# S5 scan and gated MLP on one core: a recurrence over tokens becomes a recurrence over token pairs

## The chip, the cores and the metric

The kernel runs on one core of a Trainium2 chip. The metric is the device time of one execution in microseconds (us). The engines are called as in the profile: PE is TensorE's matmuls (PEld its weight loads), DVE is VectorE, ACT is ScalarE, POOL is GpSimd, and SP is SyncE, which here only issues transfers.

## What is computed

```python
xn = layernorm(x)                              # x: 2048 tokens x 448
# branch A: a diagonal complex recurrence over the tokens, D = P = 448
Lam_bar = exp(exp(log_dt) * Lambda)            # per state p
B_bar = ((Lam_bar - 1) / Lambda)[:, None] * B  # q * B, q one complex number per state
h[t] = Lam_bar * h[t-1] + B_bar @ xn[t]
s[t] = 2 * real(C @ h[t]) + xn[t] * Dskip
# branch B: layer norm again, 448 -> 1792 -> 448
g = silu(gelu(layernorm(xn) @ w1 + b1) @ w2 + b2)
out = x + s * g
```

## The kernel before

The 2048 tokens are cut into NG = 4 groups of 512, and a group into four tiles of 128 tokens. All weights and all of x stay in SBUF. Each group goes through these steps.

- **Layer norm** (L333 to L369). Statistics on DVE; both norms (xn and the norm of xn) follow from one variance by a few short instructions (L346 to L358, on DVE for group 0, on POOL afterwards), and the scaling is on DVE for group 0, on ACT afterwards. The result is turned to columns by PE transposes in group 0 (L384) and by DMA transposes (L73) afterwards.
- **bu** (L500, L506): `B @ xn` for a block of 128 states, real and imaginary part, each four matmuls of 512 columns (K = 448 padded to 512). The 448 states are three full blocks (i = 0, 1, 2) and one block i = 3 that holds 64 real and 64 imaginary rows.
- **ssm**: a block's input is turned by a table `WT` of cosines and sines, multiplied by q (L521 to L523), so that what is left is a real decay; a DVE scan over 512 tokens (L530) runs it, once each for the real and the imaginary part; ACT casts the result (L535), and a table `VT` turns it back to h (L564 to L566). POOL turns the last column into the start value of the next group (L548 to L560).
- **mm1** (L574): a pair of 128-row blocks of the MLP's hidden layer, eight matmuls of 512 columns into two PSUM banks, then gelu on ACT (L581). Seven pairs make a group.
- **mm2** (L589, L591): for one tile, fourteen matmuls of 448 columns and one for the bias, into bank 6; tanh on ACT (L593); `g_sb` = (tanh + 1) * psum on DVE (L594).
- **ym** (L601, L603): for one tile, seven matmuls of 448 columns `C @ h` and four short ones for Dskip, into bank 7; DVE multiplies by `g_sb` (L606) and adds x (L607), and SP sends the tile out.

Nothing of this is in the order of the loops. Every step is a task of a planner (`Plan`) with an engine, the buffers it reads and writes, an assumed duration and a priority. The planner plays the tasks through with the assumed durations, and each engine's program is what came out: a fixed row in which each instruction waits for the semaphores of its inputs. What an engine does while it waits for one instruction is therefore nothing. The tables are made in the first stretch, block by block, with Sin on ACT (L438, L440), and ACT loads another table when it goes from Sin to gelu or back.

## Time and profile before

| what | us |
| --- | --- |
| median of 3 runs | 207.49 (207.39 to 207.61) |
| the profiled execution, its own time | 207.9 |
| its span, first to last instruction | 206.1 |
| PE busy | 159.0 (77%) |
| DVE busy | 154.5 (75%) |
| ACT busy | 122.5 (59%) |
| POOL busy | 44.1 (21%) |

The shares are averages over a kernel with two very different stretches, so the page's part 2, the span in forty slices, is to be read beside them: the row PE says in tenths how busy the engine was in a slice, the row PEclk which clock it was granted (9 is full speed).

### The profile page before, as it was taken

What the parts mean: (1) busy time and instruction counts of PE and PEld (TensorE: products, weight loads), DVE (VectorE), ACT (ScalarE), POOL (GpSimd) and SP (SyncE); (2) the same over time, 40 slices, a digit from 0 to 9 for tenths busy, and PEclk for the clock granted to TensorE, in tenths of its full rate; (3) what the DMA queues carried; (4) which work ended last, traced back from release to release, by engine and by line L of the source; (5) the groups of instructions that cost most, each with busy time, mean ns of one, the idle gap of its engine ahead of it and who ended that gap; (6) DMA issues with size and microseconds to landing.
All of it is one profiled execution on the core that took longest, in us unless ns stands there. A gap on an engine that the chain in (4) does not pass through costs nothing.

```text
span 206.1 us, 2551 instructions
## 1 busy us (share of the span) xinstructions
PE 159.0 (77%) x816; PEld 77.7 (38%) x816; DVE 154.5 (75%) x306; ACT 122.5 (59%) x163; POOL 44.1 (21%) x142
## 2 busy tenths in 40 slices
PE   0399339932900086999999999999999999979992
PEld 0274114310300032444544445555444555435551
DVE  6877995756699986839695857999967999935333
ACT  2366999999223089859978666543677361681110
POOL 4028200101305988850202013030410000000000
PEclk9999967996795558799999999999999999999998
DMA  5999990000000024224130500211200010100100
GB/s 168 275 282 310 285 133 0 2 0 0 0 0 2 0 50 99 60 51 104 42 73 26 102 0 0 51 48 25 70 0 3 0 36 9 48 5 0 39 28 22
DMA packets 25041, 12.61 MB, mean 61 GB/s; under 512 B 17854, under 2 KB 24675, under 8 KB 25028
## 3 DMA queue, kind: packets, MB, share of 16 engines
q1 hardware_dynamic: 24596, 10.84, 22.8%
q0 software_dynamic: 416, 1.61, 2.4%
q8 instruction: 6, 0.10, 0.2%
q14 instruction: 7, 0.06, 0.1%
q10 hardware_dynamic: 16, 0.00, 0.0%
HBM read 6.66 MB, written 1.84 MB: 41 GB/s over the span
## 4 chain that ended last, share of the span: by engine, by line
PE 61%; ACT 18%; POOL 6%; DMA 5%; DVE 4%; issue 2%; SPq 2%; DVEq 0%; ACTq 0%
PE psum L589 21%; PE psum L574 18%; PE psum L601 10%; PE psum L500 8%; DMA w_sb<-in_B_w_dram 4%; ACT L581 3%; ACT gT L581 2%; SPq L74 2%; ACT xn_sb L369 2%; ACT L438 2%; PE psum L603 2%; PE psum L591 1%; ACT tb L440 1%; PE psum L506 1%; ACT L440 1%
## 5 line engine op out<-in xcount | busy, mean ns | idle before, releaser
L589 PE MATMUL psum<-w_sb,gT 128*128 128x448 bf16 x224 | 50.7, 383 | 25.1 <-DVE g_sb L594 16.7
L574 PE MATMUL psum<-xn2T,w_sb 128*128 128x512 bf16 x224 | 53.9, 392 | 7.5 <-ACT gT L581 7.2
L589 PEld LDWEIGHTS psum<-w_sb,gT 128*128 128x128 bf16 x224 | 22.9, 105 | 50.4 <-issue 24.2
L581 ACT ACTIVATE gT<-psum 128x1024 bf16<-128x1024 f32 x28 | 28.6, 1024 | 16.2 <-PE psum L574 16.0
L574 PEld LDWEIGHTS psum<-xn2T,w_sb 128*128 128x128 bf16 x224 | 21.6, 101 | 33.7 <-ACT gT L581 8.2
L530 DVE TENSOR_TENSOR_SCAN s_f<-cw,cur,v_sb 128x512 f32<-128x512 f32 x21 | 25.9, 1270 | 0.6
L500 PE MATMUL psum<-xnT,BT 128*128 128x512 bf16 x96 | 23.3, 387 | 2.1 <-DMA xnT<-xn_sb 2.1
L601 PE MATMUL psum<-CT,h_sb 128*128 128x448 bf16 x112 | 23.8, 352 | 0.0
L593 ACT ACTIVATE th<-psum 128x448 f32<-128x448 f32 x16 | 8.6, 540 | 22.3 <-PE psum L591 22.3
L369 ACT ACTIVATE xn_sb<-x_all,lnw 128x448 bf16<-128x448 bf16 x24 | 16.7, 751 | 8.2 <-POOL lnw L358 8.2
L504 ACT ACTIVATE u_sb<-psum 128x1024 bf16<-128x1024 f32 x12 | 12.2, 1021 | 8.5 <-PE psum L500 6.6
L594 DVE SCALAR_TENSOR_TENSOR g_sb<-th,psum 128x448 bf16<-128x448 f32 x16 | 9.8, 612 | 9.1 <-ACT th L593 9.1
L535 ACT ACTIVATE s_b<-s_f 128x1024 bf16<-128x1024 f32 x12 | 12.6, 1051 | 6.0 <-DVE s_f L530 6.0
L601 PEld LDWEIGHTS psum<-CT,h_sb 128*128 128x128 bf16 x112 | 11.0, 98 | 10.6
L606 DVE TENSOR_TENSOR t<-psum,g_sb 128x448 bf16<-128x448 f32 x16 | 9.9, 619 | 6.3 <-PE psum L603 6.3
L500 PEld LDWEIGHTS psum<-xnT,BT 128*128 128x128 bf16 x96 | 9.2, 99 | 13.5 <-issue 3.0
L564 DVE TENSOR_TENSOR pa<-s_b,VT 128x1024 bf16<-128x1024 bf16 x12 | 8.2, 686 | 7.6 <-ACT s_b L535 7.6
L548 POOL TENSOR_TENSOR cwk<-s_f,rot 128x1 f32<-128x1 f32 x9 | 2.3, 252 | 50.8 <-DVE s_f L530 42.3
L568 DVE TENSOR_TENSOR pa<-s_b,QT 128x1024 bf16<-128x1024 bf16 x4 | 2.8, 692 | 10.2 <-ACT s_b L539 10.2
L396 PE MATMUL psum<-ident,gT 128*128 128x128 bf16 x28 | 3.6, 269 | 8.6 <-DMA gT<-in_A_B_re_dram 6.2
L333 DVE BATCH_NORM_STATS2 lnst<-x_all 128x6 f32<-128x448 bf16 x16 | 9.2, 614 | 0.6 <-DMA x_all<-in_A_x_dram 0.6
L522 DVE TENSOR_TENSOR pb<-u_sb,WT 128x1024 bf16<-128x1024 bf16 x12 | 8.2, 685 | 0.9 <-ACT u_sb L504 0.9
(134 smaller groups left out, 219.0 us busy)
## 6 DMA issues: line engine op xcount, KB each, us to landing
out_dram<-o_sb SPq DMA_DIRECT2D x16, 112.0 KB, 1.7
w_sb<-in_B_w_dram POOLq DMA_DIRECT2D x2, 784.0 KB, 7.9
w_sb<-in_B_w_dram SPq DMA_DIRECT2D x2, 672.0 KB, 7.8
x_all<-in_A_x_dram SPq DMA_DIRECT2D x3, 448.0 KB, 9.2
x_all<-in_A_x_dram SPq DMA_DIRECT2D x2, 224.0 KB, 2.9
gT<-in_A_B_re_dram SPq DMA_DIRECT2D x1, 336.0 KB, 4.3
...
```

Of the source, the lines that this page charges most:

```text
L333: dve(lambda e, t=t, tl=tl: e.bn_stats(lnst[:, tl, :], x_all[:, t, :]), [f"x{t}"], [f"st{tl}"], 0.56, prio)
L369: act(lambda e: e.activation(dst, x_all[:, t, :], ACT.Identity, bias=nb, scale=rs), rd, [key], 0.66, prio)
L500: fns = [lambda e, ri=ri, d=d: e.matmul(psum[:, 4 + ri, :], BT[:, d, (ri * 3 + i) * 128:(ri * 3 + i + 1) * 128], xnT[:, gx, d, :], start=( ...
L504: act(lambda e: e.activation(u_sb[:, ub, :, :], psum[:, 4:6, :], ACT.Copy), ["ps4", "ps5"], [f"u{ub}"], 1.04, prio)
L530: dve(lambda e, ri=ri, init=init: e.tensor_tensor_scan(s_f[:, ub, ri, :], col(C_R, i).to_broadcast([128, 512]), v_sb[:, ub, ri, :], init, ...
L535: act(lambda e: e.activation(s_b[:, ub, :, :], s_f[:, ub, :, :], ACT.Copy), kS, [f"sb{ub}"], 1.04, prio)
L574: fns = [lambda e, k=k, d=d: e.matmul(psum[:, b0 + k, :], w1_sb[:, d, (2 * j + k) * 128:(2 * j + k + 1) * 128], xn2T[:, gx, d, :], start=( ...
L581: act(lambda e: e.activation(gT[:, gb, 2 * j:2 * j + 2, :], psum[:, b0:b0 + 2, :], ACT.Gelu_apprx_tanh), [f"ps{b0}", f"ps{b0 + 1}"], [f"gT ...
L589: fns = [lambda e, fi=fi: e.matmul(psum[:, 6, 0:D], gT[:, gb, fi, tl * 128:(tl + 1) * 128], w2_sb[:, fi, :], start=(fi == 0), stop=False) ...
L594: dve(lambda e: e.scalar_tensor_tensor(out=g_sb[:, gs, :], in0=th[:, fb, :], scalar=1.0, in1=psum[:, 6, 0:D], op0=ALU.add, op1=ALU.mult), ...
L601: fns = [lambda e, k=k, m=m: e.matmul(psum[:, 7, 0:D], h_sb[:, hb, k, tl * 128:(tl + 1) * 128], CT[:, m, :], start=(k == 0), stop=False) f ...
L606: dve(lambda e: e.tensor_tensor(t3[:, fb, :], psum[:, 7, 0:D], g_sb[:, gs, :], ALU.mult), ["ps7", f"g{gs}"], [f"t3{fb}"], 0.6, prio)
```

## The change

With h[2k+1] = Lam² h[2k-1] + Lam B x[2k] + B x[2k+1] the state is needed at odd tokens only. So a group of 512 tokens becomes 256 pairs, and a pair's two tokens lie side by side in one partition (x is loaded so, `par` 0 is the even token).

- **bu**: the weight is `[Lam B | B]` with K = 896, seven matmuls of 256 columns for each block and part, both parts into one bank. `lb` makes Lam B in SBUF (seven `combine`s of two DVE instructions), `bt_pe` transposes seven blocks of 128 x 896.
- **ssm**: scans of 256 with the decay squared; all three full blocks go through one wide DVE instruction of 1536 elements where there were three of 1024. q has left the tables, and one table serves both turns.
- **ym**: odd tokens take `CQ` = C q at the state of their own pair and the Dskip diagonal, as before. Even tokens take `CZ` = C q Lam at the state of the pair before, and `M0`, a full 448 x 448 matrix C q B + Dskip, in place of the diagonal: eleven matmuls of 448 columns. `cq` makes CQ and CZ (seven `combine`s each, one ACT and one DVE instruction), `m0` makes M0 (four times seven matmuls of 448 columns, one short one, and an ACT copy).
- The parameters' short instructions move from DVE to POOL (`parameters`, about 50 of them in a chain), the layer norm's short ones of groups 1 to 3 from POOL to DVE (fewer of them), and the scaling of groups 1 to 3 partly from ACT to DVE.
- mm2 takes banks 5 and 6 in turn; bu takes bank 4 only; ym stays on bank 7.
- The order: the second norm and all seven mm1 of group 0 stand ahead of everything of branch A; w1 is loaded ahead of B. A DMA transpose moves 128 x 896 or 128 x 1024 at once where it moved 128 x 512. Output tiles leave in pairs, but for the last two.

```diff
+            def combine(o, a, ca, b, cb, rd, wr, prio, how="act"):
...
+                tslot[0] += 1
+                if how == "act":
+                    act(lambda e: e.activation(tmp[:, k, :], b, ACT.Copy, scale=cb), rd, [f"tmp{k}"], 0.66, prio)
+                else:
+                    dve(lambda e: e.tensor_scalar(tmp[:, k, :], b, cb, None, op0=ALU.mult), rd, [f"tmp{k}"], 0.4, prio)
+                dve(lambda e: e.scalar_tensor_tensor(out=o, in0=a, scalar=ca, in1=tmp[:, k, :], op0=ALU.mult, op1=ALU.add),
+                    rd + [f"tmp{k}"], [wr], 0.56, prio)
...
+            def lb(m, prio):
+                if m < 3:
+                    combine(Bn[:, m, 0:D], bn(m), col(LR, m), bn(m + 3), col(NLI, m), ["Bn0", "Bn1", "lr", "nli"], f"LB{m}", prio, "dve")
...
                 pe([lambda e, d=d: e.transpose(psh[:, bank, d * 128:(d + 1) * 128], Bn[:, m, d * 128:(d + 1) * 128],
-                                               ident[:, :]) for d in range(4)],
-                   rd, [f"ps{bank}"], 0.4, prio)
...
+                                               ident[:, :]) for d in range(7)], rd, [f"ps{bank}"], 0.5, prio)
...
+            def cq(dst, kd, i, r, nr, ni, pr_, rk, prio):
...
+                    combine(dst[:, 2 * i + 1, :], Cr[:, i, :], col(r, i), Cr[:, 3 + i, :], col(ni, i), CT + rk, f"{kd}{2 * i + 1}", prio)
+                    combine(dst[:, 2 * i, :], Cr[:, 3 + i, :], col(nr, i), Cr[:, i, :], col(ni, i), CT + rk, f"{kd}{2 * i}", prio)
...
+            def m0(d, bank, prio):
+                n = (128, 128, 128, 64)[d]
+                BM = (3, 0, 4, 1, 5, 2, 6)
+                fns = [lambda e, k=k, m=m: e.matmul(psum[0:n, bank, 0:D], Bn[:, m, D + d * 128:D + d * 128 + n], CQ[:, k, :],
+                                                    start=(k == 0), stop=False) for k, m in enumerate(BM)]
+                fns.append(lambda e: e.matmul(psum[0:n, bank, d * 128:d * 128 + n], ident[:, 0:n], De[:, d, 0:n], start=False, stop=True))
+                pe(fns, ["Bn0", "Bn1", "Bn60", "Bn61", "De", "ident"] + [f"CQ{k}" for k in range(7)], [f"ps{bank}"], 1.4, prio)
+                act(lambda e: e.activation(M0[0:n, d, :], psum[0:n, bank, 0:D], ACT.Copy), [f"ps{bank}", "M0p"], [f"M0{d}"], 0.58, prio)
...
             def bu(g, i, prio):
...
+                xk = [f"xnT{gx}_{b}" for b in range(2)]
+                ms = (i, 3 + i) if i < PK else (6,)
+                fns = [lambda e, r=r, m=m, d=d: e.matmul(psum[:, 4, r * NK:(r + 1) * NK], BT[:, m, d, :], xnT[:, gx, d, :],
+                                                         start=(d == 0), stop=(d == 6)) for r, m in enumerate(ms) for d in range(7)]
+                pe(fns, xk + [f"BT{m}" for m in ms], ["ps4"], 0.112 * len(fns), prio)
...
-                    fns = [lambda e, ri=ri, d=d: e.matmul(psum[:, 4 + ri, :], BT[:, d, (ri * 3 + i) * 128:(ri * 3 + i + 1) * 128],
-                                                          xnT[:, gx, d, :], start=(d == 0), stop=(d == 3))
-                           for ri in range(2) for d in range(4)]
...
+            def ssm(g, prio):
...
-                if i < PK:
-                    dve(lambda e: e.tensor_tensor(pa[:], bc(u_sb[:, ub, 0, :]), WT[:, i, 1:3, :], ALU.mult), [f"u{ub}", f"W{i}"], ["pa"], 0.66, prio)
-                    dve(lambda e: e.tensor_tensor(pb[:], bc(u_sb[:, ub, 1, :]), WT[:, i, 0:2, :], ALU.mult), [f"u{ub}", f"W{i}"], ["pb"], 0.66, prio)
-                    dve(lambda e: e.tensor_tensor(v_sb[:, ub, :, :], pa[:], pb[:], ALU.add), ["pa", "pb"], [f"v{ub}"], 0.66, prio)
...
+                dve(lambda e: e.tensor_tensor(pa[:], wide(u_sb, 0), WT[:, 0:3, 1:3, :], ALU.mult), U + WK, ["pa"], 0.96, prio)
+                dve(lambda e: e.tensor_tensor(pb[:], wide(u_sb, 1), WT[:, 0:3, 0:2, :], ALU.mult), U + WK, ["pb"], 0.96, prio)
+                dve(lambda e: e.tensor_tensor(v_sb[:, 0:3, :, :], pa[:], pb[:], ALU.add), ["pa", "pb"], ["v"], 0.96, prio)
...
+                for i in (0, 1, 2, 3):
+                    for ri in range(2 if i < PK else 1):
+                        init = 0.0 if g == 0 else cur[:, ri, i:i + 1]
+                        dve(lambda e, i=i, ri=ri, init=init: e.tensor_tensor_scan(
+                            s_f[:, i, ri, :], col(R2, i).to_broadcast([128, NK]), v_sb[:, i, ri, :], init, ALU.mult, ALU.add),
+                            [("v" if i < PK else "v3"), "r2"] + (["cur" if i < PK else "cur3"] if g else []), [f"sf{i}_{ri}"], 0.68, prio)
...
+                act(lambda e: e.activation(s_b[:, 0:3, :, :], s_f[:, 0:3, :, :], ACT.Copy), SF, ["sb"], 1.47, prio)
...
-            def mm2(t, prio):
...
-                fns = [lambda e, fi=fi: e.matmul(psum[:, 6, 0:D], gT[:, gb, fi, tl * 128:(tl + 1) * 128], w2_sb[:, fi, :],
...
+                gs, fb, bk = n % 8, n % 2, 5 + n % 2
+                fns = [lambda e, fi=fi: e.matmul(psum[:, bk, 0:D], gT[:, gb, fi, q * 128:(q + 1) * 128], w2_sb[:, fi, :],
                                                  start=(fi == 0), stop=False) for fi in range(NF)]
...
-            def ym(t, prio):
...
-                MP = [0, 3, 1, 4, 2, 5, 6]
-                fns = [lambda e, k=k, m=m: e.matmul(psum[:, 7, 0:D], h_sb[:, hb, k, tl * 128:(tl + 1) * 128], CT[:, m, :],
-                                                    start=(k == 0), stop=False) for k, m in enumerate(MP)]
-                fns += [lambda e, d=d: e.matmul(psum[:, 7, d * 128:d * 128 + VALID[d]], xnT[:, gx, d, tl * 128:(tl + 1) * 128],
-                                                Dd[:, d, 0:VALID[d]], start=False, stop=(d == 3)) for d in range(4)]
...
+            def ym(g, b, par, prio):
...
+                k0 = b * 128 + 1 + par
+                cm = (CZ, CQ)[par]
+                fns = [lambda e, k=k: e.matmul(psum[:, 7, 0:D], h_sb[:, hb, k, k0:k0 + 128], cm[:, k, :], start=(k == 0), stop=False)
+                       for k in range(7)]
+                xs = slice(b * 128, (b + 1) * 128)
+                if par == 0:
+                    fns += [lambda e, d=d: e.matmul(psum[:, 7, 0:D], xnT[:, gx, d, xs], M0[:, d, :], start=False, stop=(d == 3)) for d in range(4)]
...
+                    fns += [lambda e: e.matmul(psum[:, 7, 0:64], xnT[:, gx, 3, xs], Do[:, 0, 64:128], start=False, stop=False)]
+                    fns += [lambda e, d=d: e.matmul(psum[:, 7, 128 * d - 64:128 * d + 64], xnT[:, gx, 3 + d, xs], Do[:, d, :],
+                                                    start=False, stop=(d == 3)) for d in range(1, 4)]
...
-            ln_scale(0, "dve", -100)
...
-            for t in range(TG):
-                xt_pe(t, 0, (0, 1)[t % 2], -58, ("act", "dve")[t % 2])
...
+                    ln_apply(0, b, par, 1, "dve", -99)
+            for b in range(2):
+                xt(0, b, 1, ("act", "dve")[b], -98, bank=b)
+            parameters()
+            for j in range(7):
+                mm1(0, j, -90 + j)
+            for b in range(2):
+                for par in range(2):
+                    ln_apply(0, b, par, 0, "dve", -60)
+            for b in range(2):
+                xt(0, b, 0, "dma", -59)
...
+                lb(m, -58)
...
+                bt_pe(m, (6, 7)[m % 2], ("dve", "act")[m % 2], -57)
+            ct_dma(pr("mm1", 0))
+            for i in range(4):
+                cq(CQ, "CQ", i, QR, NQR, NQI, 1, ["qr", "nqr", "nqi", "pnqr"], 0)
+            for d in range(4):
+                m0(d, 7, 1)
+            for i in range(4):
+                cq(CZ, "CZ", i, ZR, NZR, NZI, 2, ["zr", "nzr", "nzi", "pnzr"], 2)
...
-                    ln_stats(g, pr("ln", g))
-                    ln_scale(g, "pool", pr("ln", g))
...
+                    ln_stats(g, pr("ln", g) - (40 if g == 1 else 0))
+                    ln_scale(g, pr("ln", g) - (40 if g == 1 else 0))
+                    for which in (1, 0):
+                        for b in range(2):
+                            for par in range(2):
+                                ln_apply(g, b, par, which, "dve" if g == 1 or which == 0 else "act", pr("ln", g) - (40 if g == 1 else 0))
+                            xt(g, b, which, "dma", pr("ln", g) - (40 if g == 1 else 0))
...
-                    ssm(g, i, pr("bu", g, i / 10))
-                if g == 0:
-                    ct_dma(pr("mm1", 0))
-                for j in range(7):
+                ssm(g, pr("bu", g, 1))
+                for j in range(7 if g else 0):
...
-                for tl in range(TG):
-                    t = g * TG + tl
-                    mm2(t, pr("mm2", g, tl / 2))
```

On ACT, in the first stretch, between the first copy of a bu and the fifth gelu of group 0, there stood before (gT is gelu's output, tb the tables' work buffer):

```order
L504 ACTIVATE u_sb<-psum 128x1024
L581 ACT_TABLE_LOAD
L581 ACTIVATE gT<-psum 128x1024 x2
L438 ACT_TABLE_LOAD
L438 ACTIVATE tb<-tb 128x513
L581 ACT_TABLE_LOAD
L581 ACTIVATE gT<-psum 128x1024
L481 ACTIVATE VT<-tb 128x512
L440 ACT_TABLE_LOAD
L440 ACTIVATE tb<-tb,pi 128x513
L581 ACT_TABLE_LOAD
L581 ACTIVATE gT<-psum 128x1024
```

Now the stretch from the transposed second norm to the first large table reads:

```order
L394 ACTIVATE xn2T<-psum 128x8x128
L425 ACTIVATE ang<-ang 128x8
L429 ACT_TABLE_LOAD
L429 ACTIVATE ang<-ang 128x8
L430 ACTIVATE ang<-ang,sgn 128x8
L630 ACT_TABLE_LOAD
L630 ACTIVATE gT<-psum 128x1024 x7
L524 ACTIVATE BT<-psum 128x896
L485 ACT_TABLE_LOAD
L485 ACTIVATE WT<-s_f 128x3x256
```

All seven gelus stand in one row, and the Sin instructions in two places; the loads of a table (ACT_TABLE_LOAD) in the whole program are 6 where they were 12.

On PE, up to the first output tile, there stood before:

```order
L574 MATMUL psum<-xn2T,w_sb 128x512 x8
L500 MATMUL psum<-xnT,BT 128x512 x8
L601 MATMUL psum<-CT,h_sb 128x448 x7
L603 MATMUL psum<-Dd,xnT 128x128 x3
L603 MATMUL psum<-Dd,xnT 128x64
L500 MATMUL psum<-xnT,BT 128x512 x8
L601 MATMUL psum<-CT,h_sb 128x448 x7
L603 MATMUL psum<-Dd,xnT 128x128 x3
```

Now the last rows up to the first output tile (the two lines L651 and L655) are:

```order
L637 MATMUL psum<-w_sb,gT 128x448 x14
L639 MATMUL psum<-b2blk,onesblk 128x448
L547 MATMUL psum<-CQ,Bn 128x448 x7
L549 MATMUL psum<-De,ident 128x128
L558 MATMUL psum<-xnT,BT 128x256 x7
L623 MATMUL psum<-xn2T,w_sb 128x512 x8
L547 MATMUL psum<-CQ,Bn 64x448 x7
L549 MATMUL psum<-De,ident 64x64
L623 MATMUL psum<-xn2T,w_sb 128x512 x16
L651 MATMUL psum<-CZ,h_sb 128x448 x7
L655 MATMUL psum<-M,xnT 128x448 x4
```

The first output tile now comes behind the four steps of `m0` (L547, L549), behind bu of group 1 and behind four of that group's seven mm1.

At the end of PE's program there stood before:

```order
L603 MATMUL psum<-Dd,xnT 128x128 x3
L603 MATMUL psum<-Dd,xnT 128x64
L589 MATMUL psum<-w_sb,gT 128x448 x14
L591 MATMUL psum<-b2blk,onesblk 128x448
L601 MATMUL psum<-CT,h_sb 128x448 x7
L603 MATMUL psum<-Dd,xnT 128x128 x3
L603 MATMUL psum<-Dd,xnT 128x64
```

Now there stands:

```order
L637 MATMUL psum<-w_sb,gT 128x448 x14
L639 MATMUL psum<-b2blk,onesblk 128x448
L651 MATMUL psum<-CQ,h_sb 128x448 x7
L658 MATMUL psum<-Do,xnT 128x64
L659 MATMUL psum<-Do,xnT 128x128 x3
L651 MATMUL psum<-CZ,h_sb 128x448 x7
L655 MATMUL psum<-M,xnT 128x448 x4
L651 MATMUL psum<-CQ,h_sb 128x448 x7
L658 MATMUL psum<-Do,xnT 128x64
L659 MATMUL psum<-Do,xnT 128x128 x3
```

Before, an mm2 stood between any two of the last tiles of ym; now the last three stand one behind the other, all on bank 7.

## Rows read from the trace of the kernel before

**Rows 1.** The page's part 2: forty slices of 5.15 us, busy tenths and clock.

```profile
PE   0399339932900086999999999999999999979992
...
PEclk9999967996795558799999999999999999999998
```

**Rows 2.** Two stretches: length, each engine's busy time, granted clock, DMA share, GB/s.

```profile
0.00:83.00 83.00, 40.79 (x187) 18.84 (x188) 64.96 (x172) 54.05 (x72) 27.99 (x89) 0.81 0.42 100
83.00:203.00 120.00, 118.26 (x631) 58.83 (x629) 89.09 (x134) 68.48 (x91) 16.10 (x54) 0.99 0.14 35
```

**Rows 3.** Chain of waits near 150 us: start, duration, what.

```profile
149.69 2.65 PE psum L589 x14
...
152.33 0.19 PE psum L591
...
152.52 1.73 PE psum L500 x8
...
154.25 1.73 PE psum L574 x8
...
161.40 1.32 PE psum L601 x7
...
162.73 0.20 PE psum L603 x4
```

**Rows 4.** Timeline of ACT (start, duration), and one group of its table loads.

```profile
41.15 1.28 ACT L438 ACT_TABLE_LOAD   x1
...
42.45 0.63 ACT L438 ACTIVATE tb<-tb 128x513 f32<-128x513 f32 x1
...
L581 ACT ACT_TABLE_LOAD x6 | 7.7, 1283 | 0.1
```

**Rows 5.** Who waited for whom (us in total, times, longest).

```profile
PE psum L589 <- DVE g_sb L594: 16.7, 1, 16.7
...
PE psum L589 <- ACT gT L581: 8.4, 2, 7.3
```

**Rows 6.** Timeline of PE, first 83 us (idle before, releaser).

```profile
14.43 1.90 PE L574 MATMUL psum<-xn2T,w_sb 128*128 128x512 bf16 x8 [0.34 <-DVE xn2T L392]
...
29.15 6.00 PE L574 MATMUL psum<-xn2T,w_sb 128*128 128x512 bf16 x16 [6.80 <-ACT gT L581]
...
72.96 5.38 PE L589 MATMUL psum<-w_sb,gT 128*128 128x448 bf16 x14 [16.72 <-DVE g_sb L594]
```

**Rows 7.** Timeline of DVE, the layer norm of group 0.

```profile
3.65 2.21 DVE L333 BATCH_NORM_STATS2 lnst<-x_all 128x6 f32<-128x448 bf16 x4 [0.55 <-DMA x_all<-in_A_x_dram]
...
9.21 2.54 DVE L367 TENSOR_SCALAR xn_sb<-x_all,lnw 128x448 bf16<-128x448 bf16 x8
```

**Rows 8.** Groups by line and shape: count, busy us, mean ns, idle before.

```profile
L530 DVE TENSOR_TENSOR_SCAN s_f<-cw,v_sb 128x512 f32<-128x512 f32 x7 | 8.3, 1215 | 0.0
...
L523 DVE TENSOR_TENSOR v_sb<-pa,pb 128x1024 bf16<-128x1024 bf16 x12 | 8.2, 686 | 0.1
...
L474 DVE SCALAR_TENSOR_TENSOR WT<-tb,cw 128x512 bf16<-128x512 f32 x3 | 2.2, 747 | 0.0
...
L476 DVE TENSOR_SCALAR tb<-tb,cw 128x512 f32<-128x512 f32 x3 | 1.4, 479 | 0.0
...
L404 DVE COPY BT<-psum 128x512 bf16<-128x512 bf16 x3 | 1.3, 417 | 2.1 <-PE psum L396 2.1
...
L594 DVE SCALAR_TENSOR_TENSOR g_sb<-th,psum 128x448 bf16<-128x448 f32 x16 | 9.8, 612 | 9.1 <-ACT th L593 9.1
...
L354 POOL TENSOR_TENSOR lnw<-lnw 128x8 f32<-128x8 f32 x6 | 5.1, 844 | 0.5
```

**Rows 9.** Busy time by stretch, 28 to 30 us.

```profile
28.00:30.00 2.00, 0.85 (x3) 0.30 (x4) 2.00 (x5) 1.99 (x3) 0.00 (x0) 0.50 1.18 241
```

**Rows 10.** Timeline of SP's queue: DMA transposes of group 1.

```profile
73.90 5.41 SPq L73 DMA_TRANSPOSE xnT<-xn_sb  x4
```

**Rows 11.** The chain's last steps.

```profile
202.41 0.64 DVE t L606
```

More of the change, by code (lines that the diff above doesn't have):

```diff
@@ L32 @@
 class Plan:
-    GBPS = 230.0
+    GBPS = 270.0
     def __init__(self, nc):
@@ new lines, in xt @@
+                n = (7, 8)[which]
+                key = ("xn", "xm")[which] + str(b)
+                kT = ("xnT", "xmT")[which] + f"{g % 2}_{b}"
+                oap = (xnT, xn2T)[which][:, g % 2, :, b * 128:(b + 1) * 128]
+                if how == "dma":
+                    kb.dma("sp", oap, src[:, b, :], reads=[key], writes=[kT], prio=prio, nbytes=131072, transpose=True)
+                    return
+                pe([lambda e, d=d: e.transpose(psh[:, bank, d * 128:(d + 1) * 128], src[:, b, d * 128:(d + 1) * 128],
+                                               ident[:, :]) for d in range(n)], [key, "ident"], [f"ps{bank}"], 0.08 * n, prio)
@@ new lines, in mm2 @@
+            def mm2(g, b, par, prio):
+                gb, q = g % 2, par * 2 + b
+                n = (2 * g + b) * 2 + par
+                gs, fb, bk = n % 8, n % 2, 5 + n % 2
+                fns = [lambda e, fi=fi: e.matmul(psum[:, bk, 0:D], gT[:, gb, fi, q * 128:(q + 1) * 128], w2_sb[:, fi, :],
+                                                 start=(fi == 0), stop=False) for fi in range(NF)]
+                fns.append(lambda e: e.matmul(psum[:, bk, 0:D], onesblk[:, :], b2blk[:, :], start=False, stop=True))
+                pe(fns, [f"gT{gb}_{fi}" for fi in range(NF)] + ["w2_0", "w2_1", "onesblk", "b2blk"], [f"ps{bk}"], 2.85, prio)
+                act(lambda e: e.activation(th[:, fb, :], psum[:, bk, 0:D], ACT.Tanh, scale=0.5), [f"ps{bk}"] + (WK + WKP if g == 0 else []), [f"th{fb}"], 0.58, prio - 75)
+                dve(lambda e: e.scalar_tensor_tensor(out=g_sb[:, gs, :], in0=th[:, fb, :], scalar=1.0, in1=psum[:, bk, 0:D],
+                                                     op0=ALU.add, op1=ALU.mult), [f"ps{bk}", f"th{fb}"], [f"g{gs}"], 0.62, prio - 75)
@@ L620, in pr @@
+            P = {"ln": -9, "bu": -8, "mm1": 0, "mm2": 5, "ym": 6}
             def pr(k, g, x=0.0):
```

643 lines of the change are left out of this document (312 added, 331 removed).

## The prediction

> **What bounds the kernel now.** I read the page's slices first. PE is nearly always busy from 83 us on and at full clock, and mostly waiting before [rows 1]; the two stretches in one line each say it in numbers: 118 of 120 us busy after 83 us, 41 of 83 before, at a mean clock of 0.81 [rows 2]. So there are two problems. Behind 83 us only fewer matmul columns would help; ahead of it, whatever holds PE back. The chain gives PE's prices at full clock: eight matmuls of 512 columns 1.73 us (0.216 each), fourteen of 448 2.65 (0.189 each), the bias 0.19, seven of 448 1.32, the short Dskip four 0.20 [rows 3].
>
> What holds PE back in the first 83 us is read from the timelines and waits. ACT loads a table of 1.28 us between every Sin and gelu (12 loads, six of them for gelu) [rows 4], and mm2 of group 0 needs the last gelu. Then one `g_sb` on DVE, queued behind scans, keeps the second mm2 from its bank for 16.7 us; two waits for gelu cost 8.4 [rows 5]. After such waits PE starts at half clock: sixteen matmuls took 6.00 us where 3.46 would do, fourteen took 5.38 instead of 2.65 [rows 6], with a granted 0.50, the 1.2 GHz level [rows 9].
>
> **PE's work in the changed kernel.** Per group, from the chain's prices [rows 3]: bu 49 matmuls of 256 columns at 0.108 = 5.3 us (before 28 of 512, 6.05); mm1 7 x 1.73 = 12.1; mm2 4 x 2.84 = 11.4; ym two even tiles of 11 x 0.189 = 2.08 and two odd of 1.52 = 7.2 (before 6.08). Together 35.9 us against 35.6: **PE gains nothing from the pairs**, it loses 0.3 a group. That a 256-column matmul hides its weight load isn't shown; the four short ones of at most 128 columns in 0.20 us (0.05 each) say it does, so I add nothing, and up to 0.03 each (196 of them, 6 us) as the upper bound. New on PE in the first stretch: `m0`, 4 x (7 x 0.189 + 0.05) = 5.5 us.
>
> **The start of output tiles.** The sum hangs on when the first ym can start, since PE's row behind it is nearly dense. I follow the engines.
> 1. First mm1: x arrives as before, DVE's layer norm starts at 3.65 us and its eight scalings (now four ahead of the transposes) ended at 11.75 [rows 7]; mm1 began at 14.43 [rows 6]. I keep 14.
> 2. mm1 of group 0: 12.1 us of PE, with gelus behind one Sin load and one gelu load. One bank wait of about 1 us; last gelu at 28. This takes away the table loads between gelus; six remain, 7.7 us of 15.4.
> 3. DVE from 14 us. It makes the angles and waits for Lam's parts on POOL, about 13 dependent short instructions: 0.2 us alone, 0.84 on the mean of the row where DVE ran beside it [rows 8]. I take 19 us (17 to 24). Lam B: 7 x (0.43 + 0.67), scaled to 448 elements from 0.479 and 0.747 for 512, plus four angle steps of about 0.47, = 9.6 [rows 8]. Layer norm of group 1 and the statistics of group 2, from the 8.1 us that group 0's took [rows 7], = 9.9. BT copies of 896 elements, 4 x 0.65, and one absolute value over 1024, 1.4, = 4.0. Three `g_sb` 1.8 and seven CQ of 0.67 = 6.5, and the first three wide products of 1.0 (1536 elements against 0.686 for 1024) = 3.0 [rows 8]. The last CQ is there at 19 + 9.6 + 9.9 + 4.0 + 6.5 + 3.0 = **52 us**. Seven scans of 0.64 (half of 1.215 and a little), 0.7 for block 3, two CZ, the turn back of 3 x 1.0 + 0.7, and one CZ and `g_sb` between: h of group 0 at about 64.
> 4. PE behind the last CQ: `m0` 5.5, bu of group 1 3.8, mm2 2.84, three mm1 5.2 = 17.3 us, so 69.3, and about 3 us of waits, since the copies of M0 and the gelus stand on ACT behind the cast of the scans. First ym at **72.5 us**, so PE's queue, not h, decides. Bounds: DVE without gaps and POOL at its quick end, 64.5; POOL slow and PE cold, 82.
>
> **From there to the end.** Left on PE: ym of group 0 7.2, three mm1 5.2, mm2 and ym of group 1 11.4 + 7.2, and two groups of 35.9: 102.9 us. Waits that the order puts in: DVE reads each ym out of the one bank 7 behind scans of group 1, 1 us (0 to 6); the transposes of group 2 stand on SP behind the output of group 0, and four of 8 chunks at twice the 1.35 us of a 4-chunk one [rows 10] take 10 us, so bu of group 2 waits 2.5 us (0 to 8); the last three ym stand one behind the other on one bank, where an mm2 stood between them, so twice the read of 0.64 us and its hand-over, 0.95, = 1.9. From the last ym to the span's end it was 206.1 - 202.4 = 3.7 us [rows 11]; the page's span is 1.8 us under the execution's 207.9, and this is 0.4 over the median.
>
> 72.5 + 102.9 + 5.4 + 3.7 = 184.5 us of span, + 1.8 = 186.3, - 0.4 = **186 us**. DVE's saving on scans and products, over 10 us a group, is not in this sum: behind 83 us DVE was 89 us busy in 120 [rows 2] and PE didn't wait for it. The gain is the prologue: dense work with 103 us to go starts at 72.5, where there were 119 us to go at 83.
>
> **A rule that prices the table loads otherwise.** The rows show an ACTIVATE at 42.45 right behind a load of 41.15 + 1.28 [rows 4]. The Trainium skill, page "ScalarE: Activation LUTs", section "What ACT_TABLE_LOAD costs", adds a drain of about 1380 ns to each load of 1283 ns. By it the six loads that go would give 16 us in place of 7.7; the trace shows no such drain, and I leave it out.
>
> **Rivals.**
> *A dense prologue.* DVE's short instructions overlap and POOL is quick; first ym at 64.5, and h at 58 doesn't hold it. For it: back to back, four statistics took 2.21 us [rows 7], a tenth under four single ones. Against it: the row crosses engines at every step. 64.5 + 102.9 + 3.5 + 3.7 + 1.4 = 176 to 178 us.
> *POOL's parameter chain.* At 0.84 us a step [rows 8], 13 steps are 11 us, where I count about 4; Lam's parts come 7 us later, DVE stands, and all behind it moves: 193 us. It decides if Lam B starts after 24 us. The Trainium skill, page "SBUF — State Buffer", section "Who interferes with whom", says that the two engines share a pair of ports as an exclusive lock, which speaks against moving this chain to POOL; the slow POOL rows beside a busy DVE agree with it.
> *A cold PE.* Between 32 and 41 us PE has little to do but short transposes; the clock falls, as it did before 28 us [rows 6, 9], and 20 us of work in pieces run at half speed: 10 us more, 196. The Trainium skill, page "TensorE: Matmul & The Clock Gate", Part 1, calls the lower clock the default that activity lifts. The rows show 9 from the first slice on with PE idle [rows 1], so I don't price the first mm1 at half clock; it would cost some 3 us of the same kind.
> *Slower than before.* CQ, CZ, M0 and Lam B stand in program order ahead of the first ym. If their sources (C by twelve loads and four long transposes on SP, behind everything) come so late that the first ym starts after 94 us, 103 us of PE and the waits end above 207. It takes 22 us more than I count; C's transposes would have to land after some 62 us. Price at 96 us: 210.
> *That it doesn't do what it says*: scans of 256 that cost as much as scans of 512 would add 7 x 0.6 = 4 us to step 3, inside the range.
>
> **How the numbers follow.** Forecast (181 to 190) 0.50; dense prologue 0.16; POOL 0.15; cold PE 0.14; slower 0.04; something within 0.2% 0.01. A measurement of this kernel tells about 0.2% from no change, its three runs lying within 0.1%. The range 176 to 200 holds the first four but for tails of some 0.15 in all (cold and POOL together, and a prologue still denser than the bound). Faster 0.95, same 0.01, slower 0.04.
>
> **What would show it.** First L651 near 72 us, with L547 begun near 52; seven gelus without a table load between; Lam B's first DVE instruction near 19; a granted clock of 1.00 from there on and PE busy over 95% behind it; 2 gaps of about 1 us ahead of the last two ym. Wrong, if PE still has gaps behind the first ym of more than 6 us in all, if the first ym is much later than 82, or if a 256-column matmul takes more than 0.12 us.

## The result and the profile after

The changed kernel takes **179.27 us** (median of 4 runs, 177.91 to 179.53) where the kernel before took 207.44 beside it: a ratio of 0.863, 95% interval 0.859 to 0.867. That is 28 us less; the prediction said 186 with a range of 176 to 200. The profiled execution, the quickest of them, took 177.91 us, and its span is 175.9. Where executions of one kernel lie more than 1.5% above its quickest, the ratios below leave them out, while the medians take them in.

Parts 1 and 2 of the page, which answer [rows 1]:

```profile
PE 157.7 (90%) x942; PEld 88.1 (50%) x942; DVE 116.2 (66%) x262; ACT 91.0 (52%) x137; POOL 35.7 (20%) x98
PE   0149999789989999999999999999999999999971
DVE  4798997669998997998751499611798722013342
ACT  3047659897879874757182244972326424411200
PEclk9999999999999999999999999999999999999999
```

PE is busy for 157.7 us where it was 159.0, and not busy for 18.2 us of the span where it was 47.1. So nearly all of the 30 us of span are waits that are gone. PE's busy time hides a second saving: by the prediction's count it has 6.7 us more to do (0.3 a group and 5.5 for M0) and is busy 1.3 us less. So, as an estimate, about 8 us that slow matmuls cost before (6.00 us for 3.46, 5.38 for 2.65 on [rows 6]) went too. The windows that answer [rows 2]; the columns are, for each engine, busy us and instructions, then the granted clock, the DMA share and GB/s:

```profile
0.00:20.00 20.00, 9.46 (x52) 5.05 (x53) 15.77 (x49) 8.38 (x13) 18.03 (x47) 1.00 0.95 268
20.00:40.00 20.00, 18.17 (x136) 10.95 (x134) 16.17 (x49) 15.89 (x20) 7.76 (x20) 1.00 0.84 157
40.00:60.00 20.00, 19.22 (x131) 12.43 (x130) 18.81 (x37) 16.47 (x29) 4.00 (x10) 1.00 0.28 41
60.00:80.00 20.00, 20.00 (x110) 10.04 (x108) 17.60 (x36) 13.37 (x21) 3.23 (x12) 1.00 0.03 12
80.00:176.00 96.00, 90.80 (x522) 49.69 (x520) 47.88 (x96) 36.89 (x56) 2.70 (x12) 1.00 0.17 38
```

PE is dense from 13 us on. Between 40 and 66 us DVE (third pair of numbers) is nearly as full as PE; that becomes important below. The steps that the prediction dated, from the timelines of PE, DVE and ACT:

```profile
13.00 13.53 PE L623 MATMUL psum<-xn2T,w_sb 128*128 128x512 bf16 x56 [0.98 <-DVE xn2T L396]
48.88 1.49 PE L547 MATMUL psum<-CQ,Bn 128*128 128x448 bf16 x7
67.38 1.49 PE L651 MATMUL psum<-CZ,h_sb 128*128 128x448 bf16 x7
16.56 0.51 DVE L503 TENSOR_SCALAR tmp<-Bn,cw 128x448 f32<-128x448 bf16 x1 [0.83 <-POOL cw L436]
47.49 0.68 DVE L504 SCALAR_TENSOR_TENSOR CQ<-Cr,cw,tmp 128x448 bf16<-128x448 bf16 x1
59.79 0.28 DVE L615 TENSOR_TENSOR h_sb<-pa 128x256 bf16<-128x256 bf16 x1
65.14 0.68 DVE L504 SCALAR_TENSOR_TENSOR CZ<-Cr,cw,tmp 128x448 bf16<-128x448 bf16 x1 [0.20 <-ACT tmp L501]
26.56 1.02 ACT L630 ACTIVATE gT<-psum 128x1024 bf16<-128x1024 f32 x1 [0.70 <-PE psum L623]
28.41 1.28 ACT L485 ACT_TABLE_LOAD   x1
29.70 0.84 ACT L485 ACTIVATE WT<-s_f 128x768 bf16<-128x768 f32 x1
```

All seven gelus run with no table load between. The last CZ, which an even ym needs, is ready at 65.8, only 1.6 us ahead of the first ym. PE's largest waits behind 12 us, which answer [rows 5] (us in total, times, longest):

```profile
PE psum L651 <- DVE t L663: 1.4, 2, 0.7
PE psum L558 <- ACT u_sb L562: 1.3, 2, 0.8
PE psum L623 <- DVE xn2T L396: 1.0, 1, 1.0
PE psum L637 <- ACT BT L524: 0.5, 1, 0.5
```

And three pieces of the chain, for PE's prices:

```profile
88.43 1.32 PE psum L651 x7
100.78 0.76 PE psum L655 x4
97.93 1.53 PE psum L558 x14
```

A matmul of 256 columns costs 1.53/14 = 0.109 us, its weight load (98 ns on PEld) is hidden; an even ym costs 1.32 + 0.76 = 2.08, as computed.

### The profile page after: what moved, and what is told of

Same layout as the page of the kernel before. It is cut to its first block, busy times and chain, and to the rows that moved or that the text cites. A ratio compares the mean times of both kernels' runs of the same rounds, so it can differ in the third digit from the quotient of the medians.

```text
span 175.9 us, 2656 instructions
## 1 busy us (share of the span) xinstructions
PE 157.7 (90%) x942; PEld 88.1 (50%) x942; DVE 116.2 (66%) x262; ACT 91.0 (52%) x137; POOL 35.7 (20%) x98
## 4 chain that ended last, share of the span: by engine, by line
PE 81%; ACT 8%; POOL 4%; DVE 3%; issue 1%; ACTq 0%; POOLq 0%
PE psum L623 27%; PE psum L637 23%; PE psum L651 12%; PE psum L558 10%; PE psum L655 3%; PE psum L547 2%; POOL gT L284 2%; PE psum L639 2%; DVE t L663 1%; PE psum L390 1%; ACT gT L630 1%; ACT BT L524 1%; PE psum L659 1%; ACT L630 1%; ACT L641 1%
## 5 line engine op out<-in xcount | busy, mean ns | idle before, releaser
L630 ACT ACTIVATE gT<-psum 128x1024 bf16<-128x1024 f32 x28 | 28.6, 1022 | 25.0 <-PE psum L623 24.8
L558 PE MATMUL psum<-xnT,BT 128*128 128x256 bf16 x196 | 24.0, 273 | 1.3 <-ACT u_sb L562 1.3
L558 PEld LDWEIGHTS psum<-xnT,BT 128*128 128x128 bf16 x196 | 18.8, 98 | 5.8 <-PE psum L549 1.1
L583 DVE TENSOR_TENSOR_SCAN s_f<-cw,cur,v_sb 128x256 f32<-128x256 f32 x21 | 14.5, 736 | 0.0
L651 PE MATMUL psum<-CZ,h_sb 128*128 128x448 bf16 x56 | 11.9, 353 | 0.7 <-DVE t L663 0.7
L651 PE MATMUL psum<-CQ,h_sb 128*128 128x448 bf16 x56 | 11.9, 353 | 0.7 <-DVE t L663 0.7
L562 ACT ACTIVATE u_sb<-psum 128x512 bf16<-128x512 f32 x12 | 7.1, 593 | 7.1 <-PE psum L558 7.1
L501 ACT ACTIVATE tmp<-Cr,cw 128x448 f32<-128x448 bf16 x14 | 9.2, 665 | 1.3 <-DVE CQ L504 1.2
L377 DVE TENSOR_SCALAR xn_sb<-x_all,lnw 128x448 bf16<-128x448 bf16 x24 | 8.7, 404 | 1.7 <-DMA xnT<-xn_sb 1.6
L651 PEld LDWEIGHTS psum<-CQ,h_sb 128*128 128x128 bf16 x56 | 5.4, 98 | 6.1 <-DVE t L663 1.2
L651 PEld LDWEIGHTS psum<-CZ,h_sb 128*128 128x128 bf16 x56 | 5.4, 98 | 5.9 <-DVE t L663 0.9
L587 ACT ACTIVATE s_b<-s_f 128x1536 bf16<-128x1536 f32 x4 | 5.9, 1478 | 2.9 <-DVE s_f L583 2.9
L655 PE MATMUL psum<-M,xnT 128*128 128x448 bf16 x32 | 7.4, 353 | 0.0
```

The source lines that it names most:

```text
L501: act(lambda e: e.activation(tmp[:, k, :], b, ACT.Copy, scale=cb), rd, [f"tmp{k}"], 0.66, prio)
L558: fns = [lambda e, r=r, m=m, d=d: e.matmul(psum[:, 4, r * NK:(r + 1) * NK], BT[:, m, d, :], xnT[:, gx, d, :], start=(d == 0), stop=(d == 6 ...
L583: dve(lambda e, i=i, ri=ri, init=init: e.tensor_tensor_scan(s_f[:, i, ri, :], col(R2, i).to_broadcast([128, NK]), v_sb[:, i, ri, :], init, ...
L630: act(lambda e: e.activation(gT[:, gb, 2 * j:2 * j + 2, :], psum[:, b0:b0 + 2, :], ACT.Gelu_apprx_tanh), [f"ps{b0}", f"ps{b0 + 1}"] + (WK ...
L651: fns = [lambda e, k=k: e.matmul(psum[:, 7, 0:D], h_sb[:, hb, k, k0:k0 + 128], cm[:, k, :], start=(k == 0), stop=False) for k in range(7)]
L655: fns += [lambda e, d=d: e.matmul(psum[:, 7, 0:D], xnT[:, gx, d, xs], M0[:, d, :], start=False, stop=(d == 3)) for d in range(4)]
```

## The experiments

My theory after the result was: the gain is the first stretch, and most of it is the new order there. The rival: it is the shorter recurrence on DVE. Each part was put into the kernel before by itself, then together. The kernel before was run beside each variant, with medians of 207.5 to 208.7 us; the changed kernel was not, so a difference to its 179.27 us is good to about 1 us only. A second measure leaves out the start, which differs between executions (last section): the time from the end of group 0's mm1 to the end of the span, 149.4 us in the changed kernel.

### The order alone, in the kernel before

The first edit raises the priorities of the bank readers, the second changes the order, the third does both. (The tables' code is moved behind mm1 of group 0, so that the Sin tasks can wait for its gelus; tanh of group 0 and gelu of group 1 wait for the last table, as in the changed kernel.)

```diff
-                    [f"ps{b0}", f"ps{b0 + 1}"], [f"gT{gb}_{2 * j}", f"gT{gb}_{2 * j + 1}"], 1.05, prio)
+                    [f"ps{b0}", f"ps{b0 + 1}"], [f"gT{gb}_{2 * j}", f"gT{gb}_{2 * j + 1}"], 1.05, prio - 70)
...
-                                                     op0=ALU.add, op1=ALU.mult), ["ps6", f"th{fb}"], [f"g{gs}"], 0.6, prio)
+                                                     op0=ALU.add, op1=ALU.mult), ["ps6", f"th{fb}"], [f"g{gs}"], 0.6, prio - 75)
...
-            ldb(S0 + 1)
...
+            ldw1(0, NW1, S0 + 1)
+            ldb(S0 + 5)
...
+                xt_pe(t, 1, t, -98, ("act", "dve")[t % 2])
+            for j in range(7):
+                mm1(0, j, -90 + j)
...
-                act(lambda e, R=R, SN=SN: e.activation(SN, R, ACT.Sin, scale=TWO_PI), [kR, "cr"], [kS], 0.65, TP + i)
...
+                act(lambda e, R=R, SN=SN: e.activation(SN, R, ACT.Sin, scale=TWO_PI), [kR, "cr"] + G0, [kS], 0.65, TP + i)
```

> The kernel before with one thing of the change alone: the planner's priorities of the instructions that read a PSUM bank (tanh, g_sb, gelu, the copies of u, t) are raised, so that DVE no longer runs a scan ahead of the g_sb for which a bank waits. My theory, that the gain is the first stretch and has several parts, of which the 16.7 us wait for g_sb is one: 196 to 203 us, the wait for g_sb under 6 us, the table loads still twelve or so. The rival, that the gain is the shorter recurrence on DVE: 205 to 208 us, since no work is removed and another wait takes the place.

> The kernel before with the order of the first stretch alone: w1 is loaded ahead of B, the second norm and all mm1 of group 0 stand first, the Sin tables wait for the seven gelus. The recurrence stays one over all tokens, the priorities of the readers stay low, one mm2 bank. My theory, that the order of the first stretch is most of the gain: first mm1 at 14, last gelu at 28, five or six table loads, 186 to 195 us. The rival, that the shorter recurrence and its tables on DVE decide when the first ym can start: DVE has some 20 us of tables and 22 us of recurrence ahead of h of group 0, first ym no earlier than 83, 200 us or more.

> The kernel before with the order of the first stretch and the raised priorities of the bank readers together, the recurrence still over all tokens. My theory (order is most of it): 182 to 190 us, that is 18 of the 28 us or more, PE over 90% busy from 14 us on. The rival (the halved DVE work is needed): 195 us or more, with PE's waits behind 28 us ended by DVE.

| kernel | median us | ratio to before (95%) | span | PE busy | PE not busy |
| --- | --- | --- | --- | --- | --- |
| before | 207.4 to 208.7 | 1 | 206.1 | 159.0 | 47.1 |
| readers first | 209.64 | 1.010 (1.003 to 1.017) | 209.3 | 158.6 | 50.7 |
| new order | 205.27 (201.44 to 208.63) | 0.974 (0.964 to 0.985) | 201.5 | 157.6 | 43.9 |
| both | 208.13 | 1.002 (0.998 to 1.006) | 206.0 | 156.3 | 49.7 |
| DVE's recurrence halved | 199.32 | 0.952 (0.943 to 0.961) | 197.5 | 157.3 | 40.2 |
| order, readers and halved | 191.24 | 0.918 (0.912 to 0.923) | 189.5 | 156.2 | 33.3 |
| changed kernel | 179.27 | 0.863 (0.859 to 0.867) | 175.9 | 157.7 | 18.2 |

The theory fell. The order by itself gives little and unsteadily, 2.6% with executions from 201.4 to 208.6 us, and with the readers it gives nothing. All three times miss the ranges of my theory. PE's waits with the readers first:

```profile
PE psum L500 <- DMA xnT<-xn_sb: 13.9, 1, 13.9
PE psum L589 <- DVE g_sb L594: 5.6, 3, 2.8
```

The wait of 16.7 us for `g_sb` [rows 5] is down to 5.6, and one of 13.9 for a transposed input stands in its place. With order and readers (there L534 is ym, L507 mm1, L433 bu):

```profile
PE psum L534 <- DVE h_sb L502: 14.3, 1, 14.3
PE psum L507 <- ACT gT L514: 7.4, 2, 5.0
PE psum L433 <- ACT u_sb L437: 7.0, 1, 7.0
```

The last gelu of group 0 is early there too, but then ACT and DVE make the tables, PE stands, and at the end DVE is late with h of group 3. The windows and PE's row at that place:

```profile
100.00:140.00 40.00, 39.79 (x214) 20.00 (x217) 32.64 (x50) 23.16 (x33) 5.40 (x21) 1.00 0.14 33
140.00:180.00 40.00, 35.35 (x189) 17.52 (x189) 33.53 (x52) 18.79 (x25) 3.73 (x15) 1.00 0.07 20
191.90 2.79 PE L534 MATMUL psum<-CT,h_sb 128*128 128x448 bf16 x7 [14.33 <-DVE h_sb L502]
```

DVE is busy for 33 us of 40 in both windows. From 100 us to h at 191.8 it waits for little but ACT's cast of the scans, 14.9 us in all, so it has no more to give. PE runs ahead of it until there is nothing left to do but ym, and waits 14.3 us; the next seven matmuls take 2.79 us in place of 1.49, at a granted clock of 0.50.

### Less work on DVE, without and with the order

Products and scans over half of each group's tokens, the other half of the state set to zero once:

```diff
-                    dve(lambda e, ri=ri, init=init: e.tensor_tensor_scan(s_f[:, ub, ri, :], col(C_R, i).to_broadcast([128, 512]),
-                                                                         v_sb[:, ub, ri, :], init, ALU.mult, ALU.add),
+                    dve(lambda e, ri=ri, init=init: e.tensor_tensor_scan(s_f[:, ub, ri, 0:256], col(C_R, i).to_broadcast([128, 256]),
+                                                                         v_sb[:, ub, ri, 0:256], init, ALU.mult, ALU.add),
...
```

> The kernel before in its own order, with DVE's share of the recurrence cut to half: its products and scans run over 256 of each group's 512 tokens, the other half of the state is set to zero once, so half of the recurrence is left out. PE, ACT and every matmul stay; DVE has some 11 us a group less to do. My theory, new after the orders alone gave almost nothing, is that neither part pays alone: the late start of PE stays, and the time is 194 to 203 us. The rival, that less work on DVE is the gain by itself: 190 us or less. A second rival, that neither matters and the tables' making is what counts: 204 us or more.

> The same halved recurrence on DVE (half of it is left out), in the kernel with the changed order of the first stretch and the raised priorities of the bank readers. That order with full DVE work took 208.1 us: DVE was busy 33 of 40 us behind 100 us, and PE waited 14.3 us for h of the last group. My theory, that order and shorter recurrence pay only together: 180 to 190 us, and no wait for h at the end. The rival, that the tables, made by DVE and ACT ahead of the first h, hold it: the end's wait is gone (some 12 us), the start is as late, 194 us or more.

Alone it gives 9.3 us (ratio 0.952). Its largest wait is still for `g_sb`, 13.8 us. With order and readers it gives 17.4, more than the two apart: 199.3 and 208.1 against 191.2. So they pay together, but the 180 to 190 that I expected was missed. PE's waits with all three (L510 is mm1, L436 bu, L537 ym):

```profile
PE psum L510 <- ACT gT L517: 7.4, 2, 5.4
PE psum L436 <- ACT u_sb L440: 7.0, 1, 7.0
PE psum L537 <- DVE t L542: 1.7, 1, 1.7
```

The wait for h is gone. Two kinds of wait for ACT remain, all before 62 us. They are the same as with full work on DVE, and mm1 of group 1 goes on as late (the first row is the run without the halving, the second with it):

```profile
60.66 3.60 PE L507 MATMUL psum<-xn2T,w_sb 128*128 128x512 bf16 x8 [5.05 <-ACT gT L514]
61.61 3.57 PE L510 MATMUL psum<-xn2T,w_sb 128*128 128x512 bf16 x8 [5.38 <-ACT gT L517]
```

So what the halving adds to the order comes behind 62 us. In that the rival was right, though its time (194 or more) was missed too. ACT has 24.8 us there from its last gelu of group 0 to its first tanh (33.8 to 58.6: eight Sin of 0.6 to 0.7 us, ten copies of table halves of 0.62, eight scalings of 0.75 among it); in the changed kernel that stretch is 8.7 us (27.6 to 36.3), with five Sin of 0.5 to 1.15 and no copies. Its last gelu was shown above; here are the two ends in the run with all three, and the first tanh of the changed kernel:

```profile
32.80 1.01 ACT L517 ACTIVATE gT<-psum 128x1024 bf16<-128x1024 f32 x1
58.59 0.54 ACT L529 ACTIVATE th<-psum 128x448 f32<-128x448 f32 x1
36.32 0.54 ACT L641 ACTIVATE th<-psum 128x448 f32<-128x448 f32 x1
```

The first ym is no measure across these orders. With the recurrence halved alone it starts at 74.5 us, with all three at 86.5, and yet the latter is 8 us shorter, since PE takes 119 us from there to the end of its last ym in the one and 99 in the other.

### ACT's stretch of table making

Is that stretch on the path in the changed kernel? Ten copies more ahead of the last Sin:

```diff
-                act(lambda e: e.activation(WT[:, :, 1, :], ra, ACT.Sin, scale=-TWO_PI, bias=sgn[:, 3:4]), RA + ["sgn3"], ["W1"], 1.1, TP)
+                act([lambda e, o=o: e.activation(o, ra[:, 0:2, :], ACT.Copy) for o in [s_b[:, k, :, :] for k in range(4)] + [p[:, k, :, :] for p in (pa, pb) for k in range(3)]] + [lambda e: e.activation(WT[:, :, 1, :], ra, ACT.Sin, scale=-TWO_PI, bias=sgn[:, 3:4])], RA + ["sgn3"], ["W1"], 1.1, TP)
```

> The changed kernel with ten more copies of 512 elements on ACT, about 6 us, ahead of the last Sin table, as many as the kernel before makes there from its Sin results; no engine's order changes. It asks whether the making of the tables is on the path, which would tell where the 12 us lie between the kernel with the order and the halved recurrence (191.2) and the changed one (179.3). If ACT's stretch from the last gelu to the first tanh (26.6 to 36.3) holds PE: 4 to 8 us more, 183 to 187. If PE has other work there: at most 1 us more, 180.5 or less.

185.18 us, 5.9 more (ratio 0.891, interval 0.886 to 0.896). The copies took 5.2 us, and PE's row shows where they went:

```profile
40.95 3.17 PE L558 MATMUL psum<-xnT,BT 128*128 128x256 bf16 x14 [5.68 <-ACT u_sb L562]
```

A wait of 5.68 where there was one of 0.57, and fourteen matmuls behind it in 3.17 us in place of 1.70, at a granted clock of 0.50 from 41.0 to 43.9 us. From mm1's end on it is 155.5 us, 6.1 more. So ACT's stretch counts one for one, and here the wait cost 1.5 us of slow matmuls besides.

### DVE's work put back into the changed kernel

```diff
-                        dve(lambda e, i=i, ri=ri, init=init: e.tensor_tensor_scan(
-                            s_f[:, i, ri, :], col(R2, i).to_broadcast([128, NK]), v_sb[:, i, ri, :], init, ALU.mult, ALU.add),
+                        dve([lambda e, i=i, ri=ri, init=init, o=o: e.tensor_tensor_scan(
+                            o, col(R2, i).to_broadcast([128, NK]), v_sb[:, i, ri, :], init, ALU.mult, ALU.add) for o in ([s_b[:, i, ri, :]] + ([pb[:, i, ri, :]] if i < PK else []) if g == 0 else []) + [s_f[:, i, ri, :]]],
```

The second kernel leaves out the condition on `g == 0`, so that all groups have the additional scans.

> The changed kernel, each scan of group 0 run two times more into buffers that are free then (block 3 once more): 13 scans of 0.6 us, 8 us more for DVE ahead of the first ym, no engine's order changed. My prediction said that PE's queue and not DVE decides when the first ym starts; the trace has h of group 0 at 60.1, 7 us ahead of it, but the last CZ at 65.8, 1.6 us ahead. If h is what the first ym needs last of DVE: under 2 us more, 179 to 181. If DVE as a whole, with CZ at its end, is as late as PE there: 5 to 8 us more, 184 to 187.

> The changed kernel, each scan of all groups run two times more (block 3 once more): 52 scans of 0.6 us, some 32 us more for DVE, 8 of them ahead of the first ym, no engine's order changed. DVE's work is then 148 us, near the 154 of the kernel before. If DVE has room behind the first ym, as my prediction had it: the time of the run with group 0 alone, plus at most 1 us. If DVE's load is what an early start of PE runs into: 4 to 15 us more than that run.

In group 0 alone: 185.38 us, 6.1 more. ACT's and PE's rows:

```profile
60.17 1.48 ACT L587 ACTIVATE s_b<-s_f 128x1536 bf16<-128x1536 f32 x1 [5.78 <-DVE s_f L583]
64.58 2.77 PE L547 MATMUL psum<-CQ,Bn 128*128 128x448 bf16 x7 [5.09 <-ACT M L551]
75.48 1.49 PE L651 MATMUL psum<-CZ,h_sb 128*128 128x448 bf16 x7
```

ACT's cast waits for the scans, the copy of M0 stands behind the cast, `m0` waits 5.09 us for its bank and then runs at half speed (2.77 for 1.49, granted clock 0.50). The first ym is 8.1 us later, where 13 scans at one every 0.58 us, 7.6 in all, were added; from mm1's end on it is 156.6 us, 7.2 more. In all groups: 205.07 us, 25.8 more (ratio 0.984), for 32 us more of DVE (148.2 busy against 116.2); 19.7 of the 25.8 are beyond the first run, for 25 us more of DVE in groups 1 to 3. Three of PE's rows:

```profile
82.61 2.77 PE L651 MATMUL psum<-CQ,h_sb 128*128 128x448 bf16 x7 [3.03 <-issue]
133.54 5.31 PE L623 MATMUL psum<-xn2T,w_sb 128*128 128x512 bf16 x16 [4.80 <-ACT gT L630]
160.18 1.93 PE L651 MATMUL psum<-CQ,h_sb 128*128 128x448 bf16 x7 [4.08 <-DVE t L663]
```

The first of them names no releaser, but DVE's read of bank 7, queued behind twelve scans, ended at 82.5. DVE's sum is then 148.2 us in a span of 203.3, 73%, and still PE waits for it or for ACT behind it. With nearly DVE's old load (148 of 154 us) the changed kernel is 1.6% under the kernel before (0.9 to 2.4%).

### PE's work behind the first ym

The diagonal in place of M0 in the eight even ym:

```diff
-                    fns += [lambda e, d=d: e.matmul(psum[:, 7, 0:D], xnT[:, gx, d, xs], M0[:, d, :], start=False, stop=(d == 3)) for d in range(4)]
+                    fns += [lambda e, d=d, n=n: e.matmul(psum[:, 7, d * 128:d * 128 + n], xnT[:, gx, d, xs], De[:, d, 0:n], start=False, stop=(d == 3)) for d, n in enumerate((128, 128, 128, 64))]
```

> The changed kernel, with the Dskip diagonal in place of M0 in the eight even ym, so that the term C q B x of a token's own input is left out there; M0 is still made. PE has 8 x (0.76 - 0.20) = 4.5 us less to do, and each engine's order stays. If PE's queue is what decides behind the first ym, the time falls by that 4.5 us, to 174.5 to 175.5. If DVE or a transfer decides there, by less than 2.5 us, to 177 or more.

174.7 us, 4.6 less; from mm1's end on it is 144.9 us, 4.5 less. A microsecond of PE behind the first ym is a microsecond of the kernel, as the prediction had it.

### Two small waits, and a faster version

```diff
-        psh = psum.bitcast(BF)
+        psh = psum.bitcast(BF); yb = lambda *t: 4 if t in ((3, 0, 1), (3, 1, 1)) else 7
-                cm = (CZ, CQ)[par]
+                cm = (CZ, CQ)[par]; yk = yb(g, b, par)
...
-            pool(lambda e: e.memset(Cn, 0.0), [], ["Cnp"], 2.0, S0 + 1)
...
-                         ["ident", "dcol"], ["De"], 0.6, S0 + 50)
+                         ["ident", "dcol", "pnzr", "nzi"], ["De"], 0.6, S0 + 50)
```

(The first two pairs are the two banks, where ym then uses bank `yk` for 7; the line on `Cn` is the memset; the last pair, De, and Do likewise, is in the third kernel alone.)

> The changed kernel with the second and the last of the last four ym on bank 4, which bu no longer needs, so that no ym waits for DVE to read the bank of the one before. The trace has two waits of 0.72 us there. If they are on the end's path: 1.2 to 1.5 us less, about 177.9. If the last reads on DVE decide the end anyway: no difference over 0.3 us.

> The changed kernel without POOL's memset of the buffer for C (3.51 us at 2.2 us), which is overwritten or never read in every place. In the trace the parameters' chain on POOL starts behind it, DVE's reciprocal waits 0.73 us for that chain, and the layer norm's last steps stand behind the reciprocal. If that is what holds the first mm1: 0.5 to 1.0 us less, about 178.5. If the loads of x and the parameters decide: within 0.3 us.

> The changed kernel with the last two edits together (the ym of the end on two banks, no memset of C's buffer), and the eight short products of the diagonals De and Do on POOL put behind the parameters' chain, in which they stood for about 2 us ahead of Lam. If the two small waits add up: 1.9 to 2.5 us less, 176.8 to 177.4. If Lam B, 2 us earlier, moves CQ and with it the first ym too: down to 175.5. If a later wait takes it back: 178.5 or more.

Two banks at the end: 176.91 us, ratio 0.850 (0.846 to 0.854). The last ym follow without a wait; from the end of group 0's mm1 to the end of the span it is 147.7 us where it was 149.4. That is the 1.2 to 1.5 that I expected, or a little more; the 2.4 us between the medians hold some of the starts' spread as well. Without the memset: 177.68, ratio 0.855 (0.851 to 0.860), not clear of the changed kernel's own 0.859 to 0.867. This one stays open: the reciprocal no longer waits, but in the profiled execution PE turned the parameters' rows no earlier than 6.04 us (4.89 with the memset), the first mm1 began at 12.87, only 0.13 earlier than with the memset, and from mm1's end on it is 149.3 us, as with it. All together: **175.88 us**, ratio 0.845 (0.842 to 0.849), 1.0 under the run with two banks beside it. There the first mm1 does come earlier:

```profile
12.03 8.22 PE L623 MATMUL psum<-xn2T,w_sb 128*128 128x512 bf16 x27 [0.98 <-DVE xn2T L396]
```

From mm1's end on it is 147.6 us, as in the run with two banks, so the rest of the gain lies ahead of that end. Lam B starts at 15.42 us in place of 16.56, but the first ym at 67.29 in place of 67.38. In both, group 0's mm1 ends at 26.5, since here it took 14.5 us in place of 13.5, and the first ym comes 40.8 us behind that end, so the earlier Lam B was not what decides. This version beats both kernels.

## Why the prediction was right, and where it was off

**PE's work: right.** 0.109 us for 256 columns, 2.08 and 1.52 for the two kinds of ym, 1.38 for each `m0`. From the first ym to the last one's end it is 104.9 us; without the two waits 103.4, predicted 102.9. By these prices PE gains nothing from the pairs, as predicted, and the run without M0 in ym shows that a microsecond of PE there counts in full.

**First mm1 and gelus: right.** 13.0 (predicted 14), last gelu done at 27.6 (28), six table loads. The bank wait of 1 us was not there. The slow start that I left out, because the clock's row reads full from the first slice on [rows 1], was there: mm1 of group 0 took 13.5 us where 12.1 is full speed (last section).

**DVE's list: near in its total, by luck.** Lam B began at 16.6 (19), the last CQ was done at 48.2 (52), h at 60.1 (64). 2.4 us of the 3.8 come from POOL's chain, which was done even before the 17 of its quick end. The list itself, from Lam B to the last CQ, took 31.6 us (33.0), but two errors nearly cancel in that. Its durations add up to 32.3 us, as I had them, and kept DVE busy for 27.8 only, since back to back DVE instructions follow closer than their durations: scans of 0.67 us every 0.58, wide products of 0.95 every 0.87. I had noted this [rows 7] and used it for a rival only. And DVE waited 3.8 us between them, for which my sum had nothing; these are the two largest waits:

```profile
32.11 1.23 DVE L489 SCALAR_TENSOR_TENSOR s_f<-s_f 128x1024 f32<-128x1024 f32 x1 [1.86 <-ACT WT L488]
36.89 0.62 DVE L642 SCALAR_TENSOR_TENSOR g_sb<-th,psum 128x448 bf16<-128x448 f32 x1 [1.58 <-ACT th L641]
```

**PE behind the last CQ: right to 1.3 us.** 19.2 us to the first ym (20.5). First ym at 67.4 (72.5), 5.1 early.

**Waits behind it: the term that was mis-sized.** 1.4 us in place of 5.4. The transposes of group 2 took 1.2 to 2.1 us each on SP, not the 2.5 that I took for twice [rows 10], and bu of group 2 started without a wait; t never held bank 7 behind scans. Only the two waits at the end came, 0.72 each. 5.1 + 4.0 - 0.5 of PE's work are the 8.6 us by which I was high against the profiled span; against the median of the runs it is 6.7. What happened lies between my forecast (181 to 190) and my "dense prologue" (176 to 178): the first ym came 2.9 us behind the 64.5 of that rival, and 2.1 of its 3.5 us of waits did not come.

**"The gain is the prologue": right as a place, incomplete as a cause.** I wrote that DVE's saving is not in the sum, since PE didn't wait for DVE behind 83 us [rows 2]. The sum was no worse for it, but the reading was: PE did not wait for DVE because PE itself was late. Started early, it runs into DVE's old load (14.3 us for h, and 25.8 us when most of the load is put back). And mm1 began at 14.43 before as well [rows 6]; what the order removes, DVE and ACT give back unless their own lists shrink as well: the first ym starts at 90.4 us before and at 95.3 with order and readers.

**Of the rivals**, POOL's chain held Lam B for 0.8 us only: its steps took 0.2 to 0.38 us each, not 0.84. The cold PE between 32 and 41 us did not come: the granted clock is 1.00, and fourteen matmuls of 256 columns took 1.69 or 1.70 us there, as they did later. Scans of 256 took 0.67 to 0.74 us where scans of 512 took 1.22 to 1.27, so they did get shorter. The runs show how near the cold PE was: 5 to 8 us more on ACT or DVE bring a wait of 5 us and half speed behind it. With the scans of group 0 lengthened it is the very place that the prediction named, M0's copy behind the cast.

**The page on tables.** The load at 28.41 ends at 29.69, and the Sin follows at 29.70. The Trainium skill, page "ScalarE: Activation LUTs", section "What ACT_TABLE_LOAD costs", has a drain of 1380 ns besides; this trace, like the one before, shows none.

**What stays open.** Of the 12 us between the kernel with order, readers and halved recurrence (191.2) and the changed one, the runs show that ACT's table stretch counts one for one, not how the 12 us divide between tables, scalings moved to DVE and the second mm2 bank. No run takes the new order out of the changed kernel, so what the order is worth there is argued from the other side only. That shorter transposes are what spared bu of group 2 its wait was not tested either.
